# Two attention outputs with their heads in another order, fewer weight casts, and a new fixed order of all tasks

## The chip, the core and the metric

The kernel runs on one core of a Trainium2 chip. The metric is the device time of one execution in microseconds, from launch to end; a run repeats it and the median is given. Five engines run side by side, each in the order of its own instructions: PE (matrix products; PEld is its loading of stationary operands), DVE (vector), ACT (activations), POOL (GpSimd) and SP, which here issues every DMA transfer.

## What is computed

```python
# q, k, v: (8 batches, 8 heads, 576 positions, 64), float32; scale = 1/8
scores = scale * q @ k^T
# heads 0-3: 0 <= rel < 32;  heads 4-7: 0 <= rel < 128 and rel % 4 == 0   (rel = query - key position)
attn = softmax(where(mask, scores, -1e9)) @ v
x = attn, heads side by side                      # (8, 576, 512)
gate = sigmoid(sum_k conv_w[k] * x shifted by 4-k)   # causal, 5 taps, per channel
out = (gate * (x @ w_val)) @ w_out                # (8, 576, 512) float32
```

## The kernel before

Work is cut into 753 tasks: a name, the engines that may do it, what it depends on, and the buffers ("tens") that it holds. Two strings fix everything else. `ORDER` names every task once, with the engine that does it and, behind that letter, how many *warm* matmuls on constant data PE does first (`emit`, L660). `HOMES` gives each buffer its place. `Plan.run` emits the tasks in that order, so each engine, SP's queue of transfers too, has a fixed order. A load waits for the fifth "big" load before it (`DEPTH`), and for its buffer.

Batches go in pairs g = 0..3. Task names carry a batch: `Tqd1` is the transpose of the dilated q of batch 1.

- **Loads** (SP): `Lqp`, `Lkp` (plain heads 0 to 3, L271), `Lqd`, `Lkd` (dilated heads 4 to 7, L282; in batches 0 and 7 in two pieces, the rest `Lqr`, `Lkr`), `Lvd` (v of the dilated heads, L291), `Lvp` (v of the plain heads, in parts of six blocks, L301), `Lwv`, `Lwo` (halves of the weights, L628), `Lc` (conv_w, L601).
- **Attention**: `Tqd`, `Tkd` (five transposes, L465) and `Tqp`, `Tkp` (18, L402); their copies out of PSUM `E..` on ACT or DVE (L313, L315); per unit of two heads two score halves `S` (six matmuls, L334), exponentials `E` on ACT (L341), mask multiplies `M` on DVE (L348), the output `A` (twelve matmuls, L357), and the norm `N` on DVE (L366, L367). A batch has two plain and two dilated units.
- **v**: dilated v is cast to bf16 whole (`U`, 1536 elements per partition, POOL or ACT). Plain v of batches 0 to 3 comes in its natural rows, and four groups of small casts `HA` to `HD` (2, 3, 3 and 2) move it to shifted partitions.
- **Back to channels**: `Xp` (L429) and `Xd` (L489) transpose the normed outputs, and `F` copies them to xT, in four chunks of 128 channels, two heads each.
- **Gated part**, per pair of batches and block of tokens: `C` (the convolution as products with diagonal matrices, 20 matmuls of L531; in chunks 1 and 3 the two heads swap halves on the way), `G` (tanh on ACT, L541), `V` (values, eight matmuls of L549), `Y` (their product, DVE, L559), then `O` (output, four matmuls of L578), `EO` (ACT or DVE), `ST` (store, L591).
- **Weights**: `Ct`, `Cd` make the diagonal matrices (L608 to L621). `Wv` and `Wo` cast the weights to bf16 on POOL with their rows and columns in the order of heads that xT and yT have. Before, the plain chunks of xT are heads (0, 2) and (1, 3), the dilated ones (4, 5) and (6, 7); the columns of w_val are then copied in pairs of heads, four copies for each block of rows.

PSUM has three double buffers `pd` (class ps2) and two single ones `pu` (ps1).

Of the kernel before, what the change touches and what calls it, by code (L numbers as in the profile page):

```python
# [40 lines left out]
475P 581S 467P 476A 509P 553P 540P 687P 554V 493V 696P 510V 541A 468A 497P 688A 537P 569P 570A 538A 697V 498V
684P 555P 520S 551S 519S 698S 556A 685V 668S 683S 590P 539V 592V 587P 591A 542V 518S 571V 574V 588V 511P 513P
471P 514A 472A 589A 512A 477P 690P 478V 552G 691V 517S 689S 575P 527P 530P 699P 576V 531A 584S 686S 528A 532V
702P 543P 529V 473P 544V 603P 606P 692S 585S 703A 693P 607A 700A 604A 474V 533P 469P 534V 470V 545P 605V 694V
479P 557P 583S 586S 596P 546A 480A 597A 558A 701S 705P 481P 711P 704S 706A 712A 713S 695S 708P 598V 608V 482V
609P 535P 617P 610V 625P 536A 709V 618A 593P 594A 560P 561A 717P 718A 626A 627P 562V 559V 619P 723P 620V 628V
595V 724V 611P 621P 613P 614A 622A 612V 599P 600V 714P 563P 564V 615P 616V 601P 623P 710S 707S 624V 715A 725S
602A 579P 577P 578V 637P 629P 580A 633P 634A 638A 720P 732P 721V 635P 636V 726P 727V 733A 630A 716S 719S 735P
736V 631P 728S 722S 737S 641P 639P 632V 642A 741P 729P 730A 640V 742A 734S 643P 738P 644V 731S 743S 739A 747P
740S 748A 749S 744P 745V 746S 750P 751A 752S  # L50
"""

HOMES = "01010210001103031221000021101010032002230120411231000202154111010231010110321120101271122301220031201411231212020021112110000206001103000101000002230011031001231120113230240212045111100202101001302041001671123212124101210021000010102221220222102120001100021401101302132312034023213211020202013000101100032301031101141111016210231022211200240002021121021021110220201300001302210001110013221004601212010221100130023157110003131010131221141101021013212222123004202201100111022002011222102021011203040213100310041112111410020002130114130210011312120204000311041012"
# [18 lines left out]
NAT = 4  # L72
# [85 lines left out]
def kernel(  # L158
# [72 lines left out]
    def early():  # L231
# [63 lines left out]
    def load_vp(b, ten):  # L295
        nat = b < NAT

        def issue(c):
            o = vp[ten.idx][:, c:c + 6, 0:D]
            step = 128 if nat else QB  # L300
            return nc.sync.dma_start(out=o, in_=src_ap(v, (b * H * S - (0 if nat else W) + c * step) * D,  # L301
                                                       [[D, 128], [step * D, 6], [1, D]]))
        parts = [lambda c=c: issue(c) for c in range(0, 18 if nat else 4 * NB, 6)]
        return [load(f"Lvp{b}", ten, part, big=False) for part in parts]
# [18 lines left out]
    def attend(name, u, dil, qt, kt, deps, val, v_deps, v_tens):  # L323
# [28 lines left out]
        def avm(eng):  # L352
            for j in range(NB):
                for l in range(2):
                    hf, jj = divmod(j, 3)
                    c = HW * l + QB * jj
                    nc.tensor.matmul(  # L357
                        out=ps2[po.idx][:, hf, (2 * jj + l) * DA:(2 * jj + l + 1) * DA],
                        lhsT=et[es[hf].idx][:, c:c + 128], rhs=val(j, l), start=True, stop=True)
# [15 lines left out]
    def plain(b, xb):  # L375
# [6 lines left out]
        nat = b < NAT  # L382
# [31 lines left out]
        for x in range(2):  # L414
# [7 lines left out]
            t_n, xt = attend(f"p{b}", 4 * b + x, 0, qt[x], kt[x], ee[x], val, lv + sh, [tv, tw_] if nat else [tv])  # L422
# [18 lines left out]
    def dilated(b, xb):  # L441
# [39 lines left out]
        for y in range(2):  # L481
            px = Ten("ps1")

            def trx(eng, y=y, px=px):
                o = ps1[px.idx].bitcast(BF16)
                for c in range(R):
                    for j, hb, t0 in ((0, 0, 0), (1, 1, -48), (1, 0, QB), (2, 1, 48)):
                        f = LEAD + CS * c + t0
                        nc.tensor.transpose(out=o[64 * hb:64 * hb + 64, f:f + QB],  # L489
# [107 lines left out]
    def weights():  # L597
# [14 lines left out]
        def conv_e(eng):  # L612
            for to, n, c, frm, ch in ((0, 64, 0, 0, 0), (64, 64, 0, 0, 1), (0, 64, 1, 64, 0), (64, 64, 1, 64, 1), (0, 128, 2, 0, 2)):
                w = K if c < 2 else 2 * K
                nc.vector.tensor_copy(conv_w[to:to + n].rearrange("p c k -> p (c k)")[:, K * c:K * c + w],
                                      ps1[pc.idx][frm:frm + n, K * ch:K * ch + w])
# [20 lines left out]
        for pr, parts in enumerate(((((0, 64, 0, 0, 0), (64, 64, 1, 64, 1)), ((64, 64, 0, 0, 1), (0, 64, 1, 64, 0))),  # L637
                                    (((0, 128, 0, 0, 0), (0, 128, 1, 0, 1)),))):
            t, lw = wload("wv", moe_w_val, pr)
            for part in parts:  # L640
                def cast_v(eng, t=t, pr=pr, part=part):
                    i = wt[t.idx].rearrange("p (c n) -> p c n", c=2)
                    for to, n, c, frm, ch in part:
# [3 lines left out]
        for pr, parts in enumerate((((0, 64, 0, 0, 0), (64, 64, 0, 0, 1), (0, 64, 1, 64, 1), (64, 64, 1, 64, 0)),  # L647
# [62 lines left out]
```

## Time and profile before

| what | us |
|---|---|
| median of 3 runs (lowest, highest) | 173.76 (173.69, 174.15) |
| the profiled execution | 173.49 |
| its span, first to last instruction | 171.7 |
| PE busy in the span | 154.4 |
| DVE busy | 127.7 |
| ACT busy | 105.4 |
| POOL busy | 42.2 |

The profile is of one execution; the span is 1.8 us shorter than its time. [...] Lines such as `L549 PE MATMUL pd<-xT,w_val ... x208 | 34.9, 313` give line, engine, operation, what is written from what, how often, the busy time and the mean in ns of one. A line of the time line or the chain of waits begins with its start and its length in us; brackets hold the idle time before it and what ended that.

### The profile page before, as it was taken

Reading aid. Unit: us, or ns where it says so; the run is one execution under the profiler, and the core shown is the slowest. Engines: PE = TensorE matmul, PEld = TensorE weight load, DVE = VectorE, ACT = ScalarE, POOL = GpSimd, SP = SyncE. Lnnn points to the kernel's source line nnn. Section 1 sums busy time; section 2 is a strip of 40 time slices with the busy share of each in tenths; the row PEclk is TensorE's granted clock in tenths of the full one; section 3 lists DMA queues with packets and bytes.
Section 4 is the critical chain, followed back from the end, with each engine's and each line's share of the span. In section 5 each row is a group of like instructions: output and inputs, shape, how many; then the busy total and the mean of one; then the engine's idle time right before and its main releaser. Section 6 shows DMA issues by size and latency. Waiting matters only on the chain.

```text
span 171.7 us, 5799 instructions
## 1 busy us (share of the span) xinstructions
PE 154.4 (90%) x2445; PEld 103.0 (60%) x2467; DVE 127.7 (74%) x255; ACT 105.4 (61%) x175; POOL 42.2 (25%) x77
## 2 busy tenths in 40 slices
PE   6597788799899699999997999999999999999991
PEld 1353475566666466766664656766755566785650
DVE  6607979579699998998687578979977764964521
ACT  0247776796759486888656584896675656425151
POOL 7003916998029456300000300303000000000000
PEclk9999999999999999999999999999999999999998
DMA  4999999999999917999999999980688324130645
GB/s 137 276 326 321 356 364 319 314 376 336 325 302 350 306 23 229 357 378 325 299 311 316 325 372 385 381 227 5 207 238 204 123 97 151 65 122 4 244 163 204
DMA packets 49444, 43.63 MB, mean 254 GB/s; under 512 B 23302, under 2 KB 39686, under 8 KB 49419
## 3 DMA queue, kind: packets, MB, share of 16 engines
q1 hardware_dynamic: 49418, 43.27, 80.0%
q8 instruction: 19, 0.31, 0.7%
q14 instruction: 7, 0.05, 0.1%
HBM read 33.83 MB, written 9.44 MB: 252 GB/s over the span
## 4 chain that ended last, share of the span: by engine, by line
PE 65%; DMA 13%; DVE 10%; SPq 4%; ACT 3%; issue 2%; ACTq 0%; DVEq 0%
PE pu L578 17%; PE pd L549 17%; DMA qk<-in_q_dram 10%; PE pd L531 10%; PE pd L357 5%; PE pd L334 5%; DVE xn L367 3%; PE pu L465 3%; PE pd L402 3%; PE pu L489 2%; DMA qk<-in_k_dram 2%; PE pu L429 2%; DVE et L348 2%; SPq L291 2%; SPq L301 2%
## 5 line engine op out<-in xcount | busy, mean ns | idle before, releaser
L341 ACT ACTIVATE et<-pd 128x576 bf16<-128x576 f32 x64 | 39.5, 652 | 17.2 <-PE pd L334 16.8
L348 DVE TENSOR_TENSOR et<-et,mask 128x576 bf16<-128x576 bf16 x64 | 32.2, 534 | 6.6 <-ACT et L341 6.6
L549 PE MATMUL pd<-xT,w_val 128*128 128x384 bf16 (+1 forms) x208 | 34.9, 313 | 0.2 <-ACT et L341 0.2
L578 PE MATMUL pu<-w_out,yT 128*128 128x512 bf16 x125 | 33.4, 380 | 1.5 <-issue 0.8
L367 DVE TENSOR_TENSOR xn<-pd,rec 96x768 bf16<-96x768 f32 x32 | 30.5, 954 | 1.1
L559 DVE SCALAR_TENSOR_TENSOR yT<-gate,pd 128x768 bf16<-128x768 bf16 (+1 forms) x26 | 23.0, 890 | 10.3 <-PE pd L549 9.4
L541 ACT ACTIVATE gate<-pd 128x768 bf16<-128x768 f32 (+1 forms) x26 | 19.6, 762 | 14.4 <-PE pd L531 14.2
L317 POOL CAST vn<-vd 128x1536 bf16<-128x1536 f32 x8 | 11.9, 1492 | 60.9 <-DMA vd<-in_v_dram 58.0
L549 PEld LDWEIGHTS <-w_val 128*128 128x128 bf16 x208 | 19.4, 97 | 11.3 <-issue 0.8
L531 PE MATMUL pd<-xT,conv_diag 64*64 64x384 bf16 (+1 forms) x520 | 23.7, 314 | 0.2
L585 ACT ACTIVATE osb<-pu 128x512 f32<-128x512 f32 x24 | 14.3, 599 | 10.7 <-PE pu L578 10.0
L578 PEld LDWEIGHTS <-yT 128*128 128x128 bf16 x144 | 12.6, 98 | 12.7 <-issue 0.2
L357 PEld LDWEIGHTS <-et 128*128 128x128 bf16 x384 | 15.3, 97 | 8.0 <-DVE et L348 2.1
L334 PE MATMUL pd<-qT,kT 64*128 64x96 bf16 x384 | 16.7, 207 | 3.3 <-ACT kT L313 0.6
L317 POOL CAST vw<-vp 32x384 bf16<-32x384 f32 (+2 forms) x26 | 16.0, 615 | 12.9 <-PE pu L465 7.6
L465 PE MATMUL pu<-ident,qk 128*128 128x128 bf16 x160 | 14.9, 231 | 2.4 <-DMA qk<-in_q_dram 1.4
L531 PEld LDWEIGHTS <-conv_diag 64*64 64x64 bf16 x520 | 14.2, 106 | 4.6 <-issue 0.7
L334 PEld LDWEIGHTS <-kT 64*128 64x128 bf16 x384 | 10.6, 95 | 10.6 <-issue 7.8
L465 PEld LDWEIGHTS <-qk 128*128 128x128 bf16 x160 | 10.2, 102 | 6.3 <-DMA qk<-in_q_dram 2.4
L402 PE MATMUL pd<-ident,qk 128*64 128x128 bf16 x288 | 11.1, 228 | 2.8 <-DMA qk<-in_q_dram 1.5
L315 DVE COPY xT<-pu 128x576 bf16<-128x576 bf16 x18 | 10.6, 600 | 3.9 <-PE pu L429 2.7
L402 PEld LDWEIGHTS <-qk 128*64 128x64 bf16 x288 | 9.4, 115 | 5.3 <-DMA qk<-in_k_dram 1.6
(52 smaller groups left out, 148.4 us busy)
## 6 DMA issues: line engine op xcount, KB each, us to landing
out_dram<-osb SPq DMA_DIRECT2D x36, 256.0 KB, 2.4
vd<-in_v_dram SPq DMA_DIRECT2D x8, 768.0 KB, 8.8
vp<-in_v_dram SPq DMA_DIRECT2D x28, 192.0 KB, 7.0
qk<-in_k_dram SPq DMA_DIRECT2D x8, 576.0 KB, 8.0
qk<-in_q_dram SPq DMA_DIRECT2D x8, 576.0 KB, 8.5
qk<-in_k_dram SPq DMA_DIRECT2D x6, 640.0 KB, 8.7
qk<-in_q_dram SPq DMA_DIRECT2D x6, 640.0 KB, 8.8
qk<-in_k_dram SPq DMA_DIRECT2D x2, 512.0 KB, 5.2
```

The costliest lines, as they stand in the source:

```text
L317: nc.gpsimd.tensor_copy(out_, in_)
L334: nc.tensor.matmul(out=ps2[ps.idx][:, l, QB * jj:QB * jj + QB], lhsT=kT[kt.idx][rb, c:c + 128], rhs=qT[qt.idx][rb, c:c + QB], start=True, ...
L341: nc.scalar.activation(out=et[e.idx][:, 0:2 * HW].rearrange("p (l n) -> p l n", l=2), in_=ps2[ps.idx][:, :, 0:HW], func=AF.Exp, scale=scale)
L348: (nc.vector if eng == DVE else nc.gpsimd).tensor_tensor(out=ev, in0=ev, in1=m, op=ALU.mult)
L357: nc.tensor.matmul(out=ps2[po.idx][:, hf, (2 * jj + l) * DA:(2 * jj + l + 1) * DA], lhsT=et[es[hf].idx][:, c:c + 128], rhs=val(j, l), star ...
L367: nc.vector.tensor_tensor(out=xn[xt.idx][0:QB].rearrange("p (h j) l d -> p h (j l) d", h=2), in0=a[:, :, :, 0:D], in1=rr[:, :, :, None].to ...
L402: nc.tensor.transpose(out=o[64 * y:64 * y + 64, 128 * j:128 * j + 128], in_=a[:, (y * PJ + j) * D:(y * PJ + j + 1) * D], identity=ident)
L465: nc.tensor.transpose(out=o[:, f:f + 128], in_=a[:, c * RD + 128 * cb:c * RD + 128 * cb + 128], identity=ident)
L531: nc.tensor.matmul(out=dst(ps2[pc.idx][64 * ob:64 * ob + 64, n, 0:wd]), lhsT=conv_diag[rb, 2 * cp + n, kk, :], rhs=mov(2 * cp + n, rb, c0 ...
L549: nc.tensor.matmul(out=dst(ps2[pv.idx][:, n, 0:wd]), lhsT=w_val[:, mc, c * 128:(c + 1) * 128], rhs=mov(mc, slice(0, 128), c0), start=(mc = ...
L559: nc.vector.scalar_tensor_tensor(out=yT[yb.idx][:, 2 * cp:2 * cp + 2, t0:t0 + wd], in0=gate[gt.idx][:, :, 0:wd], scalar=1.0, in1=ps2[pv.id ...
L578: nc.tensor.matmul(out=ps1[po.idx], lhsT=yT[yb.idx][:, c, c0:c0 + 128], rhs=w_out[:, c, :], start=(c == 0), stop=(c == NCH - 1))
```

## The change

It does five things.

- In a plain batch the second unit's output `A` writes its two heads in exchanged columns (`turn=x`), and in a dilated batch `Xd` writes the second chunk with exchanged halves. The chunks of xT are now heads (0, 2), (3, 1), (4, 5), (7, 6); the convolution, which swaps the halves of chunks 1 and 3, gives (0, 2), (1, 3), (4, 5), (6, 7).
- So the columns of w_val need two copies for each block of rows, each of 256 elements: 14 casts where there were 24 of 128. w_out needs five (four of 512 elements, one of 1024) where there were seven of 512. The convolution weights are copied in seven pieces instead of five.
- `NAT` becomes a tuple of the same four batches; `load_vp` gets a way to load batch 0's first plain block in two pieces, for a batch 0 that isn't in the tuple. With it come two memsets on DVE (32x64).
- `ORDER` and `HOMES` are new throughout. Tasks by engine: DVE 185 to 180, ACT 166 to 168, POOL 24 to 27. The casts `U0` and `U2` go from POOL to ACT; of the groups of shift casts POOL does 15 instead of 10 (37 casts instead of 26), ACT one instead of six. The sum of warm matmuls stays 23.
- The first loads, before: Lkd0, Lc, Lkr0, Lqd0, Lqr0, Lkp0, Lvp0, Lqp0, Lvp0, Lvd0, Lvp0, Lkd1, Lqd1, Lkd2, Lkp1, Lvd1, Lwv0, Lvp1, Lqp1, Lvp1, Lwv1, Lqd2, Lvp1, Lkp2. After: Lkr0, Lc, Lkp0, Lkd0, Lqp0, Lvp0, Lqr0, Lvp0, Lqd0, Lvp0, Lvd0, Lkd1, Lqd1, Lvd1, Lwv1, Lkp1, Lwv0, Lqp1, Lvp1, Lkd2, Lvp1, Lvp1, Lkp2, Lqd2.

PE's order at the start, up to the first plain attention output of batch 1 (Ap1; + is warm matmuls):

```
before  Tkd0+6 Ct Tqd0+1 Tkp0+2 Sd0 Sd0 Tkd0 Tqd0 Tqp0 Sd0+5 Sd0 Ad0+2 Sp0+1 Ad0+1 Tkd1 Sp0 Tkd1 Sp0 Sp0
        Tqd1 Xd0 Sd1+1 Ap0+1 Tqd1 Sd1 Ap0 Tkp1 Xd0 Sd1 Sd1 Tkd2 Xp0 C001 Tkd2 Ad1 Tqp1 Ad1 Sp1+2 Xp0 Sp1
        Sp1 Sp1 Xd1 Xd1 C000 C011 Tqd2 V001 V000 Sd2 Tqd2 Ap1+1
after   Ct Tkp0+1 Tqp0+6 Sp0+4 Tkd0 Sp0 Tkd0 Tqd0 Sd0+4 Sd0 Tqd0 Sd0+1 Ad0+4 Tkd1 Sd0 Tkd1 Ap0 Sp0 Tqd1+2
        Ad0 Sp0 Sd1 Tqd1 Sd1 Xd0 Xd0 Ap0+1 Sd1 Sd1 Tkp1 Xp0 Xp0 Ad1 C001 Ad1 Tqp1 C000 Xd1 Sp1 Sp1 Xd1
        V000 Sp1 Sp1 Tkd2 Tkd2 C011 Tkp2 V001 Tqd2 Tqd2 Ap1
```

The first tasks of POOL: before early, U0, HB0, HA0, HC0, U1, Wv0, Wv0, Wv1, HD1, HB1, Wo1, U2, HA2, HB2, Wo0, U3; after early, HB0, HC0, HA0, HD0, U1, Wv1, Wv0, Wv0, HA1, HC1, HD1, Wo0, HB2, HC2, HA2, Wo1, HD2, U3.

```diff
-NAT = 4
+NAT = (0, 1, 2, 3)
...
+            nc.vector.memset(x[0:W, 0, 0:D], 0.0)
...
-        nat = b < NAT
+        nat = b in NAT
...
+        def first():
+            return nc.sync.dma_start(out=vp[ten.idx][W:, 0, 0:D], in_=src_ap(v, 0, [[D, QB], [1, D]]))
+        rest = lambda: issue(1, 5)
...
+        if b > 0 or nat:
+            return [load(f"Lvp{b}", ten, part, big=False) for part in parts]
...
-                        out=ps2[po.idx][:, hf, (2 * jj + l) * DA:(2 * jj + l + 1) * DA],
+                        out=ps2[po.idx][:, hf, (2 * jj + (l ^ turn)) * DA:(2 * jj + (l ^ turn) + 1) * DA],
...
-                        nc.tensor.transpose(out=o[64 * hb:64 * hb + 64, f:f + QB],
+                        nc.tensor.transpose(out=o[64 * (hb ^ y):64 * (hb ^ y) + 64, f:f + QB],
...
-        def pair(a, h, step):
-            return a.rearrange("p (h d) -> p h d", d=D)[:, h:h + step + 1:step, :]
+        def cast_rows(eng, dst, i, places, turned):
+            for to, n, c, frm, ch in places:
+                o, x = dst[to:to + n, c, :], i[frm:frm + n, ch, :]
+                if turned:
+                    copy(eng, o[:, 0:4 * D].rearrange("p (b a d) -> p a b d", a=2, b=2), x[:, 0:4 * D].rearrange("p (a b d) -> p a b d", a=2, b=2))
+                    copy(eng, o[:, 4 * D:], x[:, 4 * D:])
+                else:
+                    copy(eng, o, x)
...
-                        for h, st, g, sg in ((0, 3, 0, 1), (1, 1, 2, 1), (4, 3, 4, 2), (5, 1, 5, 2)):
-                            copy(eng, pair(w_val[to:to + n, 2 * pr + c, :], h, st), pair(i[frm:frm + n, ch, :], g, sg))
+                    cast_rows(eng, w_val, wt[t.idx].rearrange("p (c n) -> p c n", c=2), part, True)
...
-                for to, n, c, frm, ch in parts:
-                    copy(eng, w_out[to:to + n, 2 * pr + c, :], i[frm:frm + n, ch, :])
+                if pr:
+                    copy(eng, w_out[:, 2:4, :], i)
+                else:
+                    cast_rows(eng, w_out, i, ((0, 64, 0, 0, 0), (64, 64, 0, 0, 1), (0, 64, 1, 64, 0), (64, 64, 1, 64, 1)), False)
```

More of the change, by code (lines that the diff above doesn't have):

```diff
@@ L47 @@
[L47 to L50, printed above, removed]
+0G 16S 1S 2P 48S 59P1 15S 3V 60V 47S 51S 56P6 57V 14S 62P4 58V 50S 13S 49S 21P 63A 65P 17S 66A 33P 53G 54G 52G
+55G 34V 31P 32A 38P4 35P 19P 22V 64V 67V 39A 36A 83S 18A 20V 40V 61V 37V 82S 26P1 41P4 42V 100P 84S 27A 28V
@@ new lines @@
+23P 88P 68P 75P 24A 7S 115S 101A 76A 85G 8G 4S 98P2 25V 29P 6G 5G 72P 69V 73A 99V 30V 105P 86P 87V 102P 89A
+106A 45P 43P 114S 74V 77V 78P1 46A 103A 107V 44A 79V 104V 118S 90P 93P 94A 91A 126P 174S 80P 70P 108P 153P 95V
+127A 128A 154A 92V 117S 96P 116S 119G 121G 122G 81V 109V 71V 97V 123P 125A 124A 149P 206S 150A 110P 139P 142P
+140A 112P 143A 151P 111V 129P 173S 152V 113A 240S 9S 130A 132P 133A 179P 180V 144V 205S 120A 131V 191P 161P
+217P 192V 218V 162A 207S 175S 155P 208S 134V 141V 219A 189P 177P 178A 190A 156V 11S 10G 145P 146V 135P 169P
@@ new lines @@
+193P 147P 170A 244P 136V 148V 194A 209S 211G 212G 210G 12G 196P 213G 181P 197A 137P 184P 241S 182A 242S 138V
+245V 185A 214P 215A 331S 273S 272S 163P 176A 171P 183V 186V 164V 256P 187P 172V 188V 216A 230P 257A 231A 165P
+166A 157P 158A 223P 224A 198V 195V 232V 199P 258P 259A 246P 159P 200V 247V 201P 203P 220P 160V 225V 221A 202V
+233P 243G 167P 222V 234A 204A 645P 646A 276S 235V 236P 168V 651P 347P 260P 261A 248P 332S 237V 249A 311P 312A
+652V 226P 238P 239A 348V 262V 251P 263P 227V 250V 648P 228P 284P 252A 264A 649A 286A 285A 253V 254P 281P 229V
@@ new lines @@
+265V 349P 255V 335P 282A 283A 266P 350A 313P 336A 267V 314V 351P 352A 300P 337P 338V 301A 268P 274S 275S 333S
+278G 354P 287P 355A 270P 288A 290P 291A 353V 307P 356V 334G 357P 289V 292V 364S 367S 309P 358V 363S 395S 650S
+308A 269A 271A 310V 302V 277G 297P 372P 374V 298A 299V 657P 373A 280G 279G 428S 293P 342P 658A 653S 339P 294V
+340A 654P 399P 368S 655A 343A 303P 369P 341V 400V 396S 366S 663P 370A 371A 664A 656S 427S 304V 365S 295P 296V
+397S 436P 378P 660P 305P 437V 438V 344V 306V 379A 661V 380V 388P 389A 375P 376A 390V 327P 328A 319P 398G 320A
@@ L295, in load_vp, with issue @@
     def load_vp(b, ten):
-        nat = b < NAT
-        def issue(c):
-            o = vp[ten.idx][:, c:c + 6, 0:D]
+        nat = b in NAT
+        def issue(c, n=6):
             step = 128 if nat else QB
-            return nc.sync.dma_start(out=o, in_=src_ap(v, (b * H * S - (0 if nat else W) + c * step) * D,
-                                                       [[D, 128], [step * D, 6], [1, D]]))
+            return nc.sync.dma_start(out=vp[ten.idx][:, c:c + n, 0:D],
+                                     in_=src_ap(v, (b * H * S - (0 if nat else W) + c * step) * D, [[D, 128], [step * D, n], [1, D]]))
+        def first():
+            return nc.sync.dma_start(out=vp[ten.idx][W:, 0, 0:D], in_=src_ap(v, 0, [[D, QB], [1, D]]))
+        rest = lambda: issue(1, 5)
         parts = [lambda c=c: issue(c) for c in range(0, 18 if nat else 4 * NB, 6)]
-        return [load(f"Lvp{b}", ten, part, big=False) for part in parts]
+        if b > 0 or nat:
+            return [load(f"Lvp{b}", ten, part, big=False) for part in parts]
+        return [load("Lvf0", ten, first, big=False), load("Lvp0", ten, rest, big=False)] + [load(f"Lvp{b}", ten, part, big=False) for part in parts[1:]]
     SHIFTS = (("HA", ((1, 0, 64, 64, 0), (1, 64, 64, 0, 1)), 1.2),
@@ L320, with attend @@
     EVS = (ACT, DVE)
[L323 removed]
+    def attend(name, u, dil, qt, kt, deps, val, v_deps, v_tens, turn=0):
         po, xt = Ten("ps2"), Ten("xn")
@@ L380, in plain @@
         lv = load_vp(b, tv)
-        nat = b < NAT
+        nat = b in NAT
         tw_, sh = Ten("vw"), []
@@ L612, in conv_e @@
         def conv_e(eng):
[L613 to L616, printed above, removed]
+            for to, n, c, frm, ch in ((0, 64, 0, 0, 0), (64, 64, 0, 0, 1), (0, 64, 1, 64, 1), (64, 64, 1, 64, 0),
+                                      (0, 128, 2, 0, 2), (0, 64, 3, 64, 3), (64, 64, 3, 0, 3)):
+                nc.vector.tensor_copy(conv_w[to:to + n].rearrange("p c k -> p (c k)")[:, K * c:K * c + K],
+                                      ps1[pc.idx][frm:frm + n, K * ch:K * ch + K])
             nc.vector.tensor_tensor(
@@ L636, in weights @@
         tw["val"], tw["out"] = [], []
-        for pr, parts in enumerate(((((0, 64, 0, 0, 0), (64, 64, 1, 64, 1)), ((64, 64, 0, 0, 1), (0, 64, 1, 64, 0))),
-                                    (((0, 128, 0, 0, 0), (0, 128, 1, 0, 1)),))):
+        for pr, parts in enumerate(((((0, 64, 0, 0, 0), (64, 64, 0, 0, 1)), ((0, 64, 1, 64, 1), (64, 64, 1, 64, 0))),
+                                    (((0, 128, 2, 0, 0), (0, 64, 3, 64, 1), (64, 64, 3, 0, 1)),))):
             t, lw = wload("wv", moe_w_val, pr)
@@ L640, in weights, with cast_v @@
             for part in parts:
-                def cast_v(eng, t=t, pr=pr, part=part):
-                    i = wt[t.idx].rearrange("p (c n) -> p c n", c=2)
-                    for to, n, c, frm, ch in part:
-                        for h, st, g, sg in ((0, 3, 0, 1), (1, 1, 2, 1), (4, 3, 4, 2), (5, 1, 5, 2)):
-                            copy(eng, pair(w_val[to:to + n, 2 * pr + c, :], h, st), pair(i[frm:frm + n, ch, :], g, sg))
+                def cast_v(eng, t=t, part=part):
+                    cast_rows(eng, w_val, wt[t.idx].rearrange("p (c n) -> p c n", c=2), part, True)
@@ L646, in weights, with cast_o @@
                 tw["val"].append(plan.add(f"Wv{pr}", (POOL,), cast_v, deps=[lw], tens=[t]))
-        for pr, parts in enumerate((((0, 64, 0, 0, 0), (64, 64, 0, 0, 1), (0, 64, 1, 64, 1), (64, 64, 1, 64, 0)),
-                                    ((0, 128, 0, 0, 0), (0, 64, 1, 64, 1), (64, 64, 1, 0, 1)))):
+        for pr in range(2):
             t, lw = wload("wo", moe_w_out, pr)
-            def cast_o(eng, t=t, pr=pr, parts=parts):
+            def cast_o(eng, t=t, pr=pr):
                 i = wt[t.idx].rearrange("p (c n) -> p c n", c=2)
-                for to, n, c, frm, ch in parts:
-                    copy(eng, w_out[to:to + n, 2 * pr + c, :], i[frm:frm + n, ch, :])
+                if pr:
+                    copy(eng, w_out[:, 2:4, :], i)
+                else:
+                    cast_rows(eng, w_out, i, ((0, 64, 0, 0, 0), (64, 64, 0, 0, 1), (0, 64, 1, 64, 0), (64, 64, 1, 64, 1)), False)
```

51 lines of the change are left out of this document (19 added, 32 removed).

## The prediction

> **What bounds the kernel now.** I read the page first: shares of the engines, the slices, and the chain that ended last.
>
> ```profile
> span 171.7 us, 5799 instructions
> PE 154.4 (90%) x2445; PEld 103.0 (60%) x2467; DVE 127.7 (74%) x255; ACT 105.4 (61%) x175; POOL 42.2 (25%) x77
> PE   6597788799899699999997999999999999999991
> DMA  4999999999999917999999999980688324130645
> GB/s 137 276 326 321 356 364 319 314 376 336 325 302 350 306 23 229 357 378 325 299 311 316 325 372 385 381 227 5 207 238 204 123 97 151 65 122 4 244 163 204
> PE 65%; DMA 13%; DVE 10%; SPq 4%; ACT 3%; issue 2%; ACTq 0%; DVEq 0%
> ```
>
> A slice is 4.29 us. PE is nearly full from slice 15 on; from slice 2 to 14 the transfers are full. So the kernel is a start fed by transfers, then a long stretch set by PE. A busy PE is not a dense one, so I took from the chain of waits (start, us, what) what each step costs where PE runs without a gap:
>
> ```profile
> 63.00 0.26 PE pu L429 x6
> 64.20 0.62 PE pd L402 x18
> 66.45 0.37 PE pd L357 x12
> 66.82 0.28 PE pu L465 x5
> 67.10 1.30 PE pd L549 x8
> 68.40 0.36 PE pd L334 x12
> 68.76 0.80 PE pu L489 x32
> 69.82 0.94 PE pd L531 x20
> ```
>
> With the code's names: a dilated transpose task Td (L465) is 0.28, a plain one Tp (L402) 0.62, a score half S (six matmuls of L334) 0.18, an attention output A (L357) 0.37, the transposes back Xp (L429) 0.26 and Xd (half of the L489 row) 0.40, a convolution C (L531) 0.94, a value block V (L549) 1.30. I call **lag** the time at which PE starts a task less the dense work that the order puts ahead of it. PE has the same tasks in both kernels, and each lists 23 warm matmuls, so a smaller lag at the same work is time gained, if nothing takes it back. The lines of time of PE (start, length, what, idle before it):
>
> ```profile
> 9.97 1.17 PE L402 MATMUL pd<-ident,qk 128*64 128x128 bf16 x18 [0.37 <-DMA qk<-in_k_dram]
> 17.07 0.53 PE L357 MATMUL pd<-vn,et 128*128 128x65 bf16 x12 [0.66 <-POOL vn L317]
> 30.96 0.69 PE L402 MATMUL pd<-ident,qk 128*64 128x128 bf16 x18 [1.50 <-DMA qk<-in_q_dram]
> 36.82 2.76 PE L549 MATMUL pd<-xT,w_val 128*128 128x384 bf16 x16
> 40.35 0.35 PE L357 MATMUL pd<-vw,et 128*128 128x65 bf16 x6
> 58.25 0.24 PE L357 MATMUL pd<-vw,et 128*128 128x65 bf16 x2 [1.26 <-DVE et L348]
> ```
>
> Two points matter. **Point 1** is Tqp1, the last q transpose of batch 1, at 30.96. Ahead of it: 10 Td, 3 Tp, 12 S, 5 A, 2 Xd, 1 Xp, 1 C = 10.7 us, so the lag is 20.3. **Point 2** is the first plain attention output of batch 1, at 40.35. Ahead: 12 Td, 4 Tp, 17 S, 6 A, 4 Xd, 2 Xp, 3 C, 2 V = 18.7, lag 21.7. So over half of the first 40 us is lost to PE.
>
> **The change part by part.** *Bytes.* At the start a load lands when the bytes ahead of it have moved. Sizes:
>
> ```profile
> vd<-in_v_dram SPq DMA_DIRECT2D x8, 768.0 KB, 8.8
> vp<-in_v_dram SPq DMA_DIRECT2D x28, 192.0 KB, 7.0
> qk<-in_k_dram SPq DMA_DIRECT2D x8, 576.0 KB, 8.0
> qk<-in_k_dram SPq DMA_DIRECT2D x6, 640.0 KB, 8.7
> qk<-in_k_dram SPq DMA_DIRECT2D x2, 512.0 KB, 5.2
> ```
>
> Summing the GB/s line, 1730 KB have moved at 8.6 us, 3095 at 12.9, 4440 at 17.2, 5930 at 21.5, 7456 at 25.8, 8790 at 30.0, 10105 at 34.3, 13088 at 42.9. Check: the k load of plain batch 0 ends the first 1866 KB, moved at 9.0; PE used it at 9.97, 0.9 later. The q load of plain batch 1 ends 8330 KB, moved at 28.6, used at 30.96, 2.4 later. So a landing is the moved bytes plus 0.9 to 2.4. The other sizes stand in the code: half a weight matrix 512 KB, a rest 128. The new order of loads, in running KB: k rest 128, conv_w 138, kp0 714, kd0 1226, qp0 1802, then three parts of vp0, q rest and qd0 up to 3018, vd0 3786, kd1 4426, qd1 5066, vd1 5834, wv1 6346, kp1 6922, wv0 7434, **qp1 8010**, vp1 and kd2 up to 9226, kp2 9802, up to vd2 13130.
>
> *Point 1 in the new order.* Ahead of Tqp1 now: 8 Td, 3 Tp, 12 S, 6 A, 2 Xd, 2 Xp, 1 C = 10.7. Its load is 320 KB earlier, so it lands at 27.5 plus 0.9 to 2.4: 28.4 to 29.9, a lag of 17.7 to 19.2 where it was 20.3. The transfers offer 1.1 to 2.6.
>
> *What could stop PE from being there.* The first cast of dilated v (U0) goes from POOL to ACT, where it stands behind two exponentials, and U2 goes the same way. ACT's nearest rows:
>
> ```profile
> L541 ACT ACTIVATE gate<-pd 128x768 bf16<-128x768 f32 x18 | 14.6, 813 | 5.9 <-PE pd L531 5.6
> L313 ACT CAST vw<-vp 32x384 bf16<-32x384 f32 x10 | 5.2, 516 | 0.2
> ```
>
> A U has 1536 elements per partition: more than the 813 ns of 768, and at most, in proportion, twice that, 1626 ns, or four times the cast row, 2064. I take 1.5, as an instruction has a part that doesn't grow. vd0 lands at 15.1 plus 0.9 to 2.4, U0 ends at 17.5 to 19.6, and the first Ad0 (17.07 before, 3.1 us of work ahead; now 3.3) is 0.4 to 2.5 later. Queued behind U0 on ACT are two exponentials, a k copy and two plain exponentials, for which the mask multiplies and A tasks wait. But from Ad0 to Tqp1 PE has 7.4 us of work and 9 to 12 us of time, so this wait is hidden in the wait for qp1; without that cover it costs up to 2.5.
>
> *Casts.* The POOL rows, by shape, then two stretches of its time line:
>
> ```profile
> L317 POOL CAST vn<-vd 128x1536 bf16<-128x1536 f32 x8 | 11.9, 1492 | 60.9 <-DMA vd<-in_v_dram 58.0 <-PE pd L334 2.7
> L317 POOL CAST vw<-vp 32x384 bf16<-32x384 f32 x18 | 11.2, 625 | 4.9 <-PE pu L429 3.9 <-DMA vp<-in_v_dram 0.2
> L317 POOL CAST w_out<-wt 64x512 bf16<-64x512 f32 x6 | 3.8, 632 | 0.3
> 17.08 5.24 POOL L317 CAST vw<-vp 32x320 bf16<-32x320 f32 x8
> 28.68 6.90 POOL L317 CAST w_val<-wt 64x128 bf16<-64x128 f32 x24
> ```
>
> w_val: 24 casts of 128 elements, 6.90/24 = 0.29 each, become 14 of 256. A 256 one lies between 0.29 and the 0.63 of 512; on the line between them 0.40, so 5.6 us, a gain of 1.3 (bounds: gain 2.8, loss 1.9, if a 256 cost as little as a 128 or as much as a 512). w_out: 7 casts become 4 of 512 and one of 1024 (between 0.63 and 1.49, say 1.06): 3.6 for 4.4. POOL's total is off the path, but its first part is not: the values begin at 36.82 and the w_val casts end at 35.58. In the new order wv1 is cast first, wv0 lands at 25.7 plus 0.9 to 2.4 and its 8 casts end at 29.8 to 31.3; the first value block stands 2.7 us of work behind Tqp1, at 31.1 to 32.6. So the casts cease to hold the values, and C and V of batch 0 fill what was idle.
>
> *Shifts.* POOL takes all four of batches 0, 2, 3 and three of batch 1: 37 casts for 26, ACT 3 for 14. POOL: 11 x 0.62 - 2 x 1.49 - 2.1 = +1.7 us; ACT: -11 x 0.52 + 2 x 1.5 = -2.7. For point 2 the last vp1 part is 9226 KB, moved 31.4, landed 32.3 to 33.8, then 7 casts at 5.24/8 = 0.66: 36.9 to 38.4.
>
> *Point 2 in the new order.* Ahead: 12 Td, 5 Tp, 16 S, 6 A, 4 Xd, 2 Xp, 3 C, 2 V = 19.1, that is 8.4 behind Tqp1: 36.8 to 38.3 if dense, hardly later by the shifts, and up to 1.5 later if DVE, which the attention of batch 0 and 1 keeps full, is late with norms. I take 38.7: lag 19.6 for 21.7, **2.1 us gained** (bounds 0.8 to 4.0).
>
> *Afterwards.* U2 on ACT needs vd2: moved 43.0, cast by 45.4 to 46.9; Ad2 stands behind 25.9 of work, at 45.5. At worst its lag is 21.0, still under the 21.7 of point 2 before. Then PE's idle time is small:
>
> ```profile
> 55.00:60.00 5.00, 3.69 (x53) 2.12 (x48) 4.97 (x8) 2.52 (x5) 2.78 (x3) 1.00 1.06 315
> 60.00:75.00 15.00, 14.84 (x270) 10.24 (x273) 14.15 (x27) 12.18 (x21) 6.52 (x9) 1.00 0.71 222
> 75.00:100.00 25.00, 23.21 (x421) 15.93 (x424) 18.76 (x36) 16.85 (x28) 1.47 (x1) 1.00 1.08 324
> 100.00:165.00 65.00, 64.07 (x965) 42.97 (x973) 47.25 (x82) 37.28 (x63) 2.94 (x2) 1.00 0.54 180
> ```
>
> (Busy us of PE, PEld, DVE, ACT, POOL.) From 60 to 165 PE idles 2.9. The whole order is new there; I have no row for its waits, and bound them by none (2.9 gained) and by twice as many (2.9 lost), and take them as they are.
>
> *At nothing.* The exchange of heads leaves the number of matmuls and transposes; the conv_w copies, 7 for 5, and two short memsets on DVE lie ahead of the first scores, under the first transfers, which PE waits for until 9.97; uncovered, under 0.5 us at the durations of DVE's short copies. The tuple NAT names the same four batches; the two-part first load is not reached. The last tasks, V331 and four outputs, stand as before.
>
> **Sum.** 173.49 (span 171.7 and 1.8 around it) - 2.1 = 171.4. The median of the runs shown, 173.76, is 0.27 above the profiled execution; I say 171.5.
>
> **The rivals.** *(a) Larger.* DVE has five tasks fewer, and two of the long casts leave POOL. The 1.26 us wait at 58.25 and half of the 2.9 go too: 171.5 - 2.7 = 168.8. Against it: U3, beside that wait, stays on POOL.
>
> *(b) No change.* From 55 to 75 DVE idles 0.9 of 20 us. If it sets the pace there, not PE, an earlier PE only waits: 173.5. Against it: the new order has no more DVE work ahead of the values of that time than the old one.
>
> *(c) Slower.* The mask multiply (L348) against POOL's casts:
>
> ```profile
> L348 DVE TENSOR_TENSOR et<-et,mask x64: 440/449/1712, 12.5 to 146.8; 128x576 bf16<-128x576 bf16 x64
> 19.55 0.45 DVE L348 TENSOR_TENSOR et<-et,mask 128x576 bf16<-128x576 bf16 x1
> 56.31 1.58 POOL L317 CAST vn<-vd 128x1536 bf16<-128x1536 f32 x1
> 56.48 1.71 DVE L348 TENSOR_TENSOR et<-et,mask 128x576 bf16<-128x576 bf16 x1
> ```
>
> The one at 56.48 took 1.71 for a median of 0.45 and ended shortly after the cast that ran beside it. If each of the 11 added shift casts holds a multiply for its whole 0.62, DVE gets 6.8 us more, less 2 x 1.26 for the U casts gone: 4.3, all before 65 us, where DVE is full. It decides above 2.1, what was gained: 173.5 + 2.2 = 175.7. Against it: the multiply at 19.55 ran amid the 5.24 us of shift casts from 17.08, and took 0.45.
>
> [...]
>
> **Chances.** Forecast 0.55 (its own range 170.0 to 172.9), (a) 0.14, (b) 0.12, (c) 0.19. Range 169.0 to 174.8: it leaves out the far ends of (a) and (c). Faster by over 0.3% (0.52 us, about what a measurement tells apart) 0.68, within 0.11, slower 0.21.
>
> **What would show it.** Tqp1 at 28.4 to 30 instead of 30.96, the first value block before 34 instead of 36.82, Ap1 of the first half before 39.5, PE idle of about 3 us from 60 to 165. Wrong, if qp1 lands as late as before, if L348's mean rises well over 534 ns, or if PE's idle time after 60 us grows by more than 2.

## The result, and the profile after

The changed kernel takes 172.3 us in the median of six runs (169.99 to 173.36), the kernel before on the same chip 173.85 (173.67 to 174.45). The ratio is 0.986 with an interval of 0.982 to 0.990; it leaves out two runs of the changed kernel above 1.5% over its fastest, 173.23 and 173.36, and over all runs the means give 0.989. The profiled execution took 169.99, the fastest of the six, so its trace shows more gain (3.5 us) than the median (1.6).

The page of the changed kernel: span, busy time, two rows of the slices, the chain's shares:

```profile
span 168.3 us, 5815 instructions
PE 153.1 (91%) x2467; PEld 102.1 (61%) x2467; DVE 123.8 (74%) x254; ACT 104.7 (62%) x171; POOL 45.0 (27%) x74
PE   0977597999999999999999999999999999999991
DMA  4999999999999999985999769996595612061645
...
PE 63%; DVE 12%; POOL 8%; DMA 7%; SPq 4%; ACT 2%; issue 2%; POOLq 0%; DVEq 0%; ACTq 0%
```

A slice is 4.21 us. PE is full from slice 8 on (29.5 us), before nearly full from slice 15 (60.1 us). How much of the 3.4 us that the span lost is idle time of PE can't be read from the busy times (153.1 for 154.4): the trace of before has 2445 of the 2467 matmuls. In the chain that ended last (the lowest line) transfers have 7% for 13, and POOL, which was not in it, has 8. POOL works 2.8 us more, where 1.7 were forecast.

The line of time of PE (start, length, what, idle before it), the two points of the prediction and what lies between:

```profile
17.89 0.55 PE L363 MATMUL pd<-vn,et 128*128 128x65 bf16 x12 [0.57 <-DVE et L354]
20.86 0.22 PE L363 MATMUL pd<-vw,et 128*128 128x65 bf16 x2 [1.39 <-POOL vw L323]
...
27.72 0.69 PE L408 MATMUL pd<-ident,qk 128*64 128x128 bf16 x18 [0.97 <-DVE xn L373]
30.76 0.69 PE L408 MATMUL pd<-ident,qk 128*64 128x128 bf16 x18
33.60 1.47 PE L555 MATMUL pd<-xT,w_val 128*128 128x384 bf16 x8
...
39.64 0.23 PE L363 MATMUL pd<-vw,et 128*128 128x65 bf16 x2
...
56.30 0.22 PE L363 MATMUL pd<-vw,et 128*128 128x65 bf16 x2 [0.40 <-POOL vw L323]
```

Tqp1 starts at 30.76 (30.96 before), and nothing that it waits for is named: its load was there. The first value block is at 33.60 (36.82), Ap1 at 39.64 (40.35), Ap2 at 56.30 (58.25). In lags, with the work ahead that the prediction lists, for this trace: point 1 is 30.76 - 10.7 = 20.1 for 20.3, point 2 is 39.64 - 19.1 = 20.5 for 21.7.

Stretches of the same kernel (us, then busy us and instructions of PE, PEld, DVE, ACT, POOL, then granted clock, DMA share, GB/s):

```profile
24.00:30.00 6.00, 4.56 (x115) 3.76 (x119) 5.93 (x13) 4.79 (x9) 5.79 (x10) 1.00 1.10 340
60.00:75.00 15.00, 14.39 (x264) 9.81 (x264) 13.36 (x25) 12.87 (x23) 7.02 (x11) 1.00 1.04 333
75.00:100.00 25.00, 24.68 (x427) 16.60 (x428) 19.71 (x38) 17.80 (x29) 1.47 (x1) 1.00 0.82 249
100.00:165.00 65.00, 64.62 (x945) 42.34 (x937) 43.73 (x75) 36.59 (x62) 3.50 (x2) 1.00 0.60 198
```

From 60 to 165 PE idles 105 - 103.69 = 1.3, for 2.9 before. But matmuls that a trace lacks count as idle time. The rows of the output matmuls on the two pages, before and after (count, busy us, mean ns, idle time ahead of them):

```profile
L578 PE MATMUL pu<-w_out,yT 128*128 128x512 bf16 x125 | 33.4, 380 | 1.5 <-issue 0.8
L584 PE MATMUL pu<-w_out,yT 128*128 128x512 bf16 x144 | 36.0, 380 | 0.3 <-ACT xT L319 0.3
```

Before, 19 of 144 are missing, and 1.5 of the 2.9 lie ahead of this line, in gaps of 0.05 to 0.16. What is left, 1.4, is about what PE idles after the change: this stretch had little to give. From 24 to 30, ahead of point 1, it is DVE that is full: 5.93 of 6 (5.72 before).

The line of time of POOL (start, length, what, idle before it):

```profile
14.00 6.81 POOL L323 CAST vw<-vp 32x320 bf16<-32x320 f32 x10 [9.64 <-DMA vp<-in_v_dram]
23.63 1.46 POOL L323 CAST vn<-vd 128x1536 bf16<-128x1536 f32 x1 [2.82 <-DMA vd<-in_v_dram]
25.04 7.09 POOL L323 CAST w_val<-wt 128x256 bf16<-128x256 f32 x14
...
56.31 1.47 POOL L323 CAST vn<-vd 128x1536 bf16<-128x1536 f32 x1
```

Ten shift casts end at 20.81, and the first Ap0 waits for them until 20.86. U3 is the cast at 56.31; it matters below.

### The profile page after: what moved, and what is told of

The parts are those of the page before. It is cut to its first block, busy times and chain, and to the rows that moved or that the text cites. A ratio compares the mean times of both kernels' runs of the same rounds, so it can differ in the third digit from the quotient of the medians.

```text
span 168.3 us, 5815 instructions
## 1 busy us (share of the span) xinstructions
PE 153.1 (91%) x2467; PEld 102.1 (61%) x2467; DVE 123.8 (74%) x254; ACT 104.7 (62%) x171; POOL 45.0 (27%) x74
## 4 chain that ended last, share of the span: by engine, by line
PE 63%; DVE 12%; POOL 8%; DMA 7%; SPq 4%; ACT 2%; issue 2%; POOLq 0%; DVEq 0%; ACTq 0%
PE pu L584 18%; PE pd L555 13%; PE pd L537 10%; POOL vw L323 7%; DMA vp<-in_v_dram 7%; PE pd L363 5%; PE pd L340 5%; PE pd L408 4%; DVE et L354 4%; DVE xn L373 3%; SPq L283 3%; PE pu L471 3%; PE pu L495 3%; DVE yT L565 2%; PE pu L435 2%
## 5 line engine op out<-in xcount | busy, mean ns | idle before, releaser
L584 PE MATMUL pu<-w_out,yT 128*128 128x512 bf16 x144 | 36.0, 380 | 0.3 <-ACT xT L319 0.3
L354 DVE TENSOR_TENSOR et<-et,mask 128x576 bf16<-128x576 bf16 x64 | 30.8, 514 | 0.9 <-ACT et L347 0.8
L323 POOL CAST vw<-vp 32x384 bf16<-32x384 f32 (+2 forms) x37 | 22.0, 595 | 22.3 <-DMA vp<-in_v_dram 16.4
L537 PE MATMUL pd<-xT,conv_diag 64*64 64x384 bf16 (+1 forms) x520 | 22.8, 313 | 0.3 <-DVE yT L565 0.2
L591 ACT ACTIVATE osb<-pu 128x512 f32<-128x512 f32 x21 | 12.5, 601 | 15.8 <-PE pu L584 13.5
L323 POOL CAST vn<-vd 128x1536 bf16<-128x1536 f32 x6 | 9.4, 1562 | 47.9 <-DMA vd<-in_v_dram 26.5
L593 DVE TENSOR_SCALAR osb<-pu 128x512 f32<-128x512 f32 x15 | 10.2, 684 | 7.3 <-PE pu L584 4.9
L471 PE MATMUL pu<-ident,qk 128*128 128x128 bf16 x160 | 13.6, 220 | 0.6 <-DMA qk<-in_q_dram 0.6
L372 DVE RECIPROCAL rec<-pd 96x12 f32<-96x12 f32 x32 | 7.2, 225 | 9.0 <-PE pd L363 7.9
L321 DVE COPY xT<-pu 128x576 bf16<-128x576 bf16 x16 | 8.4, 527 | 5.6 <-PE pu L435 3.3
```

What stands on the lines that cost most here:

```text
L323: nc.gpsimd.tensor_copy(out_, in_)
L354: (nc.vector if eng == DVE else nc.gpsimd).tensor_tensor(out=ev, in0=ev, in1=m, op=ALU.mult)
L471: nc.tensor.transpose(out=o[:, f:f + 128], in_=a[:, c * RD + 128 * cb:c * RD + 128 * cb + 128], identity=ident)
L537: nc.tensor.matmul(out=dst(ps2[pc.idx][64 * ob:64 * ob + 64, n, 0:wd]), lhsT=conv_diag[rb, 2 * cp + n, kk, :], rhs=mov(2 * cp + n, rb, c0 ...
L584: nc.tensor.matmul(out=ps1[po.idx], lhsT=yT[yb.idx][:, c, c0:c0 + 128], rhs=w_out[:, c, :], start=(c == 0), stop=(c == NCH - 1))
```

## The experiments

All ratios are to the kernel before, run on the same chip beside it; its medians were 173.38, 173.43 and 173.52 in the three sets.

### The heads alone, the order alone

```diff
 heads_only:  code of the changed kernel
+ORDER, HOMES = those of the kernel before
 order_only:  code of the kernel before (24 and 7 weight casts)
+ORDER, HOMES = those of the changed kernel
```

> The changed kernel's code (heads exchanged, fewer weight casts, two memsets) with the old ORDER and HOMES. My theory, that the gain comes from the order alone: within 0.5 us of the kernel before (173.3 to 174.4). Rival, that fewer weight casts free POOL and DVE: 0.6 to 2 us faster, with the last w_val cast earlier than 35.58 us.

> The old code (24 and 7 weight casts, heads as before) with the new ORDER and HOMES. My theory: as fast as the changed kernel, within 0.6 us (171.0 to 172.5). Rival, that the casts matter: slower than the changed kernel by 0.6 to 2 us, with the last w_val cast later than 32.1 us and the first value block behind it.

heads_only: 174.08 (172.54 to 174.82), ratio 1.002 [1.000, 1.005]. order_only: 171.0 (169.99 to 172.92), 0.985 [0.981, 0.988]. POOL's lines of time, first of heads_only, then of order_only:

```profile
28.80 3.69 POOL L323 CAST w_val<-wt 64x256 bf16<-64x256 f32 x8
33.21 2.35 POOL L323 CAST w_val<-wt 128x256 bf16<-128x256 f32 x6 [0.72 <-DMA wt<-in_moe_w_val_dram]
```

```profile
23.98 8.55 POOL L317 CAST w_val<-wt 128x128 bf16<-128x128 f32 x24
33.01 3.59 POOL L317 CAST vw<-vp 64x384 bf16<-64x384 f32 x6 [0.48 <-DMA vp<-in_v_dram]
```

In the old order 14 casts take 6.04 us for 6.90, but POOL waits 0.72 between them for the second half of the weights and ends at 35.56 for 35.58: nothing is gained. In the new order 24 casts take 8.55, 14 take 7.09; the first value block was at 32.95 with 24, and at 33.60 and 32.90 in two traces with 14. So the whole gain is the order's. The exchange of heads, with its fewer casts, saves POOL 0.9 to 1.5 us that nothing waits for.

### The changed kernel again

> The changed kernel once more, for the spread of its times (170.0 to 172.3 so far). If the spread is one of the start, a profile of a longer execution has the same distances between PE's tasks after 60 us and a later first value block (33.6 us in the profile so far); if it is one of the whole run, the distances grow everywhere.

171.56 (170.74 to 173.49), 0.990 [0.986, 0.994]. The profiled span was 171.1, 2.8 more than in the first trace, but its start is the earlier one: the first value block is at 32.90 for 33.60, Ap2 at 55.97 for 56.30. So the spread is not one of the start. Two points of PE's start, then what differs later, in the lines of time of DVE, POOL and PE of this run:

```profile
29.99 0.69 PE L408 MATMUL pd<-ident,qk 128*64 128x128 bf16 x18
...
38.94 0.22 PE L363 MATMUL pd<-vw,et 128*128 128x65 bf16 x2
```

```profile
54.96 2.27 DVE L354 TENSOR_TENSOR et<-et,mask 128x576 bf16<-128x576 bf16 x2
...
86.98 2.09 DVE L354 TENSOR_TENSOR et<-et,mask 128x576 bf16<-128x576 bf16 x2
```

```profile
55.36 1.57 POOL L323 CAST vn<-vd 128x1536 bf16<-128x1536 f32 x1
...
87.13 1.63 POOL L323 CAST vn<-vd 128x1536 bf16<-128x1536 f32 x1 [17.94 <-DMA vd<-in_v_dram]
```

```profile
57.29 0.30 PE L363 MATMUL pd<-vw,et 128*128 128x65 bf16 x4 [0.97 <-DVE et L354]
...
91.05 1.02 PE L584 MATMUL pu<-w_out,yT 128*128 128x512 bf16 x3 [1.45 <-ACT xT L319]
```

Here U3 starts at 55.36, amid two mask multiplies that take 2.27 us together; U5 at 87.13 meets another two, 2.09 (two undisturbed ones take 0.82, as the next test shows). PE waits 0.97 in Ap2 and 1.45 after 89. In the first trace the multiplies near U3 were over before it started, and PE's second wait was short; the lines of DVE and PE there:

```profile
54.58 1.30 DVE L354 TENSOR_TENSOR et<-et,mask 128x576 bf16<-128x576 bf16 x2
```

```profile
88.19 1.02 PE L584 MATMUL pu<-w_out,yT 128*128 128x512 bf16 x4 [0.32 <-ACT xT L319]
```

The multiplies ended at 55.88, U3 came at 56.31. The two waits are 2.1 us longer in the second trace (0.97, and 1.45 for 0.32), of the 3.1 that it loses behind Ap2. A POOL that is 0.9 us earlier goes with a slower kernel, and this is a guess at why its runs lie 3 us apart. The next test takes both casts from POOL.

### U3 and U5 to ACT

```diff
-234A 204A 645P 646A 276S        243G (U3) six tasks earlier
+234A 204A 645P 646A 243A 276S
-434A 360A 362A 381P             398G (U5) earlier
+434A 360A 362A 398A 381P
```

> The changed kernel with the casts U3 and U5 (1536 elements per partition) moved from POOL to ACT, U3 behind the first output copy, U5 behind the two xT copies of batch 4. Theory of the long casts: a mask multiply on DVE that meets one waits for its end; in the longer execution of the changed kernel U3 (55.36) and U5 (87.13) each held one to 1.7 us. Then no multiply near 55 and 87 us is over 0.9 us, and the median falls by 0.5 to 1.5 us to 170.0 to 171.0. Rival, that the spread has another source, or that ACT's 1.5 us each cost as much: 171.3 or more, same spread.

170.13 (169.87 to 170.7), 0.982 [0.980, 0.984]: 1.4 us under the changed kernel's 171.56, and all runs within 0.8. DVE's and PE's lines of time at the same places:

```profile
55.18 1.01 DVE L321 TENSOR_TENSOR et<-et,mask 128x576 bf16<-128x576 bf16 x2
84.97 0.82 DVE L321 TENSOR_TENSOR et<-et,mask 128x576 bf16<-128x576 bf16 x2
```

```profile
56.31 0.34 PE L330 MATMUL pd<-vw,et 128*128 128x65 bf16 x6
...
87.91 1.02 PE L551 MATMUL pu<-w_out,yT 128*128 128x512 bf16 x3 [0.32 <-ACT xT L286]
```

Neither pair takes over 1.01, and of PE's two waits the first is gone and the second down to 0.32. (A multiply at 53.47 still took 1.12, beside the w_out cast of 1024 elements.) So the two casts on POOL cost time, and by these four runs they made most of the spread.

### HD0 to ACT as well

```diff
-54G 52G 55G (HD0) 34V
+54G 52G 34V
-100P 84S 27A 28V
+100P 84S 27A 55A 28V
```

> As u35_act, and the last shift group of batch 0 (HD0, two casts) moved from POOL to ACT behind the third dilated exponential. Theory that POOL's ten serial casts set the first plain attention output (1.39 us of waiting at 20.86): Ap0's second part starts 0.8 to 1.2 us earlier, Tqp1 0.5 to 1 us earlier, and the time is 0.3 to 1.0 us under u35_act. Rival, that DVE's norms and multiplies set Tqp1 anyway: Ap0 earlier, Tqp1 and the time the same within 0.3 us.

169.53 (169.47 to 170.15), 0.979 [0.977, 0.981]; and on another chip

> u35_hd0 once more, beside the next run: 169.5 to 170.2 us, ratio to the kernel before 0.977 to 0.981.

169.52 (169.2 to 170.04), 0.977 [0.975, 0.979]. This is the best version, 4 us under the kernel before. But not as expected; PE's line of time of the second run:

```profile
19.14 0.39 PE L330 MATMUL pd<-vw,et 128*128 128x65 bf16 x6
...
26.89 0.69 PE L375 MATMUL pd<-ident,qk 128*64 128x128 bf16 x18 [0.97 <-DVE xn L340]
29.93 0.69 PE L375 MATMUL pd<-ident,qk 128*64 128x128 bf16 x18
```

Ap0 no longer waits for POOL, yet Tqp1 is at 29.93, and at 29.99 in the first run (29.69 in u35_act, where POOL still has HD0): PE stands behind the norms of DVE (0.97 at 26.89). By the medians the kernel is 0.6 us shorter all the same; the intervals of u35_act and u35_hd0 overlap a little (0.980 to 0.984, 0.977 to 0.981), and where the 0.6 comes from stays open.

### The same order with the old heads

```diff
 u35_hd0_oldheads:  ORDER, HOMES of u35_hd0
+code of the kernel before (24 and 7 weight casts)
```

> The order of u35_hd0 with the old code: heads as before, 24 and 7 weight casts. Theory that the fewer casts save POOL 0.9 to 1.5 us that hardly anything waits for: within 0.4 us of u35_hd0_b. Rival, that they matter once the long casts are out of the way: 0.5 to 1.5 us slower, with the first value block behind the casts.

170.06 (169.31 to 170.31), 0.979 [0.977, 0.982]. The interval overlaps that of u35_hd0_b on the same chip (0.975 to 0.979): what the casts are worth is not told apart from nothing, and is about half a microsecond by the medians.

### U0 and U2 back on POOL

```diff
-36A 83S 18A (U0) 20V            -272S 163P 176A (U2) 171P
+33P 18G 53G 54G                 +194A 209S 176G 211G
```

> The changed kernel with U0 and U2 back on POOL, U0 ahead of the shift casts of batch 0 and U2 ahead of those of batch 2. Theory that moving these casts off POOL is part of the gain: the shift casts of batch 0 start at about 17.5 instead of 14.0 us, Ap0 ends 3 us later, Tqp1 at 32 to 34 instead of 30 to 30.8, and the time is 1 to 3 us over the changed kernel (172.5 to 174.5). Rival, that the later slack hides it: within 0.5 us of the changed kernel.

174.73 (173.95 to 175.62), 1.008 [1.005, 1.011]. POOL's and PE's lines of time:

```profile
16.00 1.47 POOL L290 CAST vn<-vd 128x1536 bf16<-128x1536 f32 x1 [11.63 <-DMA vd<-in_v_dram]
17.52 6.67 POOL L290 CAST vw<-vp 32x320 bf16<-32x320 f32 x10
```

```profile
23.10 0.27 PE L330 MATMUL pd<-vw,et 128*128 128x65 bf16 x2 [2.58 <-POOL vw L290]
24.25 0.27 PE L330 MATMUL pd<-vw,et 128*128 128x65 bf16 x2 [0.88 <-POOL vw L290]
...
25.96 0.74 PE L438 MATMUL pu<-ident,qk 128*128 128x128 bf16 x5 [0.22 <-issue]
```

The shift casts, ready at 14, start at 17.52 behind U0, and Ap0 waits 3.5 us. Without these two moves the new order is slower than the old. U0 and U2 were moved together, so their shares are not told apart; the rows shown are of U0 alone.

### The loads alone, the engines alone

```diff
 old_loads:            changed kernel
+first 24 loads in the order of before
 new_loads_old_order:  kernel before
+first 24 loads in the order of the changed kernel
```

> The changed kernel with the first 24 loads in the old order (k of dilated batch 0 first, q of plain batch 1 behind 8330 KB instead of 8010), every other engine's order as changed. Theory that the new order of transfers carries the gain of the start: Tkp0 at 10 instead of 5.3 to 6.3, Tqp0 at 12, shift casts from 16 instead of 14, Tqp1 1.5 us or more later, the time 1 to 2.5 us over the changed kernel. Rival, that DVE and POOL set Tqp1 and the transfers have slack: within 0.5 us.

> The kernel before with the first 24 loads in the new order, every other engine's order as before. Theory that loads and engine orders only gain together: PE's first task, the k transpose of dilated batch 0, waits for 1226 KB instead of 512 (7 us instead of 4.9), Tqp1 at 30 to 31.5, the time 0 to 2 us over the kernel before. Rival, that the transfers alone carry the gain: 1 to 2 us faster than before.

176.35 (174.37 to 177.12), 1.013 [1.009, 1.017], and 177.5 (176.19 to 178.61), 1.022 [1.018, 1.025]. Each half alone is slower than the kernel before, and both by more than was expected: some 4 us over the kernel that each was made from. PE's line of time of each, old_loads first:

```profile
38.36 2.74 PE L522 MATMUL pd<-xT,w_val 128*128 128x384 bf16 x8 [2.53 <-POOL w_val L290]
```

```profile
12.92 0.72 PE L432 MATMUL pu<-ident,qk 128*128 128x128 bf16 x5 [4.68 <-DMA qk<-in_q_dram]
```

With the old loads the weights come too late for the early values (2.53 at 38.36); with the new loads the old PE order asks first for a dilated q that now comes late (4.68 at 12.92).

### Six more warm matmuls

```diff
+            for h in range(6):
+                nc.tensor.matmul(out=ps1[pc.idx], lhsT=warm[:, 0:128], rhs=warm, start=True, stop=True)
```

> The changed kernel with six warm matmuls more, ahead of the conv_w transposes at the start of PE's order, as the old order had them. If the spread of the changed kernel's times comes from PE's rate in its first 15 us: times at 170 to 171 with a spread under 1 us. If not: the median and the spread stay, 171 to 172.3.

171.9 (171.64 to 172.6), 0.991 [0.989, 0.994], where the changed kernel had 0.990. So PE's rate in its first microseconds isn't what holds the start. In this trace too a multiply was long: 1.67 us at 54.71, for 0.45 in the median; U3 is at 55.36 and 56.31 in the two of the changed kernel.

## Why the prediction was right, and where it wasn't

The forecast was 171.5 for the median and 171.4 for the profiled execution, 2.1 us less than before. The median measured is 172.3; the ratio times the median of before is 0.986 x 173.85 = 171.4, and the runs lie on both sides of it. The place named first, the start, is where the order gains. That the sum came so near is in part luck. The gain at Ap1 was 1.2 in the first trace and 1.8 in the second, at Ap2 3.0 and 3.3, where the forecast had no more than at Ap1; behind Ap2 the second trace lost 2.7 of it again, where it had nothing. By its steps:

- **Point 1: wrong in what sets it.** The prediction had Tqp1 wait for its load, with a gain of 1.1 to 2.6. In neither trace of the changed kernel does it wait for a load; its lag fell by 0.2 in the first (30.76) and by 1.0 in the second (29.99). The prediction costed the work between Ad0 and Tqp1 as 7.4 us of PE in 9 to 12 us of time with slack to spare; in the first trace it took 12.9 us (17.89 to 30.76). First Ap0 waited 1.39 for the ten shift casts of batch 0, where the prediction had worked out only those of batch 1; then PE waited 0.97 for a norm of DVE, ahead of Tkp1. Taking HD0 from POOL removed the first wait and left Tqp1 where it was, so DVE is the one that ends last. And in the first trace DVE was itself held: of three mask multiplies that stand before that norm the first ran beside U1, still on POOL (23.63 to 25.09), and took 1.11. The three in that trace, then in u35_act, where U1 was over at 23.95 and Tqp1 came at 29.69:

```profile
24.30 2.24 DVE L354 TENSOR_TENSOR et<-et,mask 128x576 bf16<-128x576 bf16 x3
```

```profile
23.98 1.18 DVE L321 TENSOR_TENSOR et<-et,mask 128x576 bf16<-128x576 bf16 x3
```

  A lag counts PE's work alone, and says nothing of an engine that fills up between two points.
- **Point 2: right in kind, too large.** In the first trace 1.2 us gained (20.5 for 21.7) where 2.1 was forecast, inside its bounds of 0.8 to 4.0; in the second Ap1 was at 38.94 for a forecast of 38.7, 1.8 gained. Of the 1.2 in the first, 0.2 came at point 1 and 1.0 behind it, where C and V of batch 0 fill PE as predicted: from Tqp1 to Ap1 it takes 8.9 us for 8.4 of work, before 9.4 for 8.0. The first value block started at 33.60, before the 34 that was to show it, though not at 31.1 to 32.6.
- **U0 on ACT: right.** 1.474 us in the mean for 1.5 (0.517 for a cast of 384 elements), and Ad0 at 17.89 lies in 17.5 to 19.6. That it was worth so much (1.8% between u02_pool and after_again, together with U2) was not said; it had been costed only as a possible delay, not as what frees POOL for the shift casts.
- **Weight casts: a smaller gain than costed, and worth nothing that the runs tell apart.** w_val 6.04 us in the old order and 7.09 in the new for an estimate of 5.6, within its bounds; w_out 2.60 + 1.14 = 3.7 for 3.6. That they cease to hold the values is so, but by the order: 24 casts do not hold them either.
- **Afterwards: about unchanged in the median, as taken, but not in its parts.** Half of the 2.9 that PE idled is missing records, so the bounds worked out from it were twice too wide. In the first trace the wait of 1.26 in Ap2 fell to 0.40, which is the other part of rival (a), and its 169.99 lies between (a) and the forecast. In the second trace Ap2 waits 0.97 again. At Ap2 the work ahead is 33.0 before and 34.0 after, at the prediction's durations, so the lag went from 25.3 to 22.3 in the first trace and to 22.0 in the second: of the first's 3.5 us, 1.8 came between Ap1 and Ap2.
- **Rival (b)** fails: in the first trace PE idles no more after 60 us than before. In the second it does, but its longest wait is the one behind U5, and DVE, which by (b) sets the pace there, is busy 12.49 of 15 us from 60 to 75. **Rival (c)** named the right effect, a multiply that takes longer beside a cast, and the wrong casts. Beside the narrow casts a multiply took 0.60 in the mean of 23 (0.54 of 17 before, 0.45 alone, by the casts that overlap each multiply in the two traces): 0.15 each, not a whole cast. Beside the 1536-element casts 0.67 in the first trace, for 1.00 of seven before, since only by luck none met U3 (one met U1, at 24.30); in the second trace it was up to 1.72. The groups of the first and the second trace (busy us, mean ns), then the same line of the second (shortest, median and longest in ns):

```profile
L354 DVE TENSOR_TENSOR et<-et,mask 128x576 bf16<-128x576 bf16 x64 | 30.8, 514 | 0.9 <-ACT et L347 0.8
L354 DVE TENSOR_TENSOR et<-et,mask 128x576 bf16<-128x576 bf16 x64 | 33.0, 545 | 1.5 <-ACT et L347 1.3
```

```profile
L354 DVE TENSOR_TENSOR et<-et,mask x64: 441/451/1718, 13.4 to 144.3; 128x576 bf16<-128x576 bf16 x64
```

The mean was 534 before; it fell to 514 in the first trace and rose to 545 in the second. (c), with 4.3 us more over 64 multiplies, needed about 600.

The term of (c), a narrow cast that holds a multiply for its whole 0.62, no run shows: in the first trace and in that of before the longest multiply beside narrow casts took 0.77, 0.32 over one alone, and the 0.15 in the mean is a quarter of a narrow cast (0.58 in the mean of the first trace). The two 1536-element casts that met multiplies in the second trace, of 1.57 and 1.63, go with the 1.72. It can be the cast that takes longer: in the first trace the one at 117.48 took 2.03 us where five others took 1.46 to 1.47, and the multiply at 117.73, inside it, 0.44. What decides between the two was not shown.

## What to carry to other kernels

Where loads and engines follow one written order, neither half can be judged alone: both halves of this change lose (ratios 1.013 and 1.022), together they win (0.990). A lag of the bound engine is a good measure at a point, but ahead of it look at which other engine is full in that stretch. When runs of one kernel spread, compare a short and a long trace: here long GpSimd casts that did or did not meet mask multiplies account for most of the difference (2.1 of 3.1 us), and moving two such casts to ACT gave more (1.4 us by the medians) than all of the fewer casts (about 0.5). Before you read idle time from two traces, compare their counts of instructions: here missing matmuls made half (1.5 of 2.9 us) of what looked like waiting.

## What the runs showed of the hardware

In two runs in which PE waited long at the start, the granted clock was lower as well. Stretches of new_loads_old_order, and below them one of u02_pool, with the columns as before; the granted clock is the third figure from the end:

```profile
8.00:16.00 8.00, 3.32 (x38) 2.05 (x37) 2.04 (x5) 1.81 (x2) 0.00 (x0) 0.51 1.15 314
16.00:24.00 8.00, 7.53 (x107) 4.93 (x102) 6.02 (x10) 6.01 (x11) 7.46 (x10) 0.85 1.08 365
```

```profile
24.00:32.00 8.00, 6.35 (x115) 5.17 (x118) 6.18 (x12) 4.84 (x9) 7.60 (x16) 0.74 1.14 325
```

In new_loads_old_order PE was busy 3.32 of 8 us, and the granted clock was 0.51 there and still 0.85 in the next 8, with PE busy 7.53; in u02_pool it was 0.74 after Ap0's wait, and the five transposes at 25.96 took 0.74 us, where five of them took 0.45 at 20.00, before that wait. The changed kernel keeps 1.00 in all of its first 58 us; old_loads has 0.85 from 32 to 41, where PE waits 2.53. So part of what old loads, new loads and u02_pool lose may be this, and was not separated from the waits. Not every wait goes with a lower figure: old_loads, with PE busy 1.10 of its first 8 us and a wait of 4.11 up to 9.95, has 1.00 up to 32. Nor does the column show every slow stretch: in the kernel before it reads 1.00 from 8 to 16, yet there the 18 transposes at 9.97 took 1.17 us, for 0.69 at 30.96; in the changed kernel those at 9.84 took 0.69 already.
